# First pass of a gated feed-forward layer made with seven products instead of eight, during attention

## The chip, the cores and the metric

The kernel runs on one core of one Trainium2 chip. The time is device microseconds of one execution, and the figure used is the median of several. A profile of one execution stands beside the times. TensorE multiplies matrices (PE in the profile; PEld is its loading of weights), VectorE (DVE) and ScalarE (ACT) read its results out of PSUM, GpSimd (POOL) works on SBUF alone, and SyncE (SP) issues the transfers.

## The reference

Attention over a window, and its output through a gated layer of two matrix steps. All numbers are fp32.

```python
scores = scale * np.matmul(q, k.transpose(0, 1, 3, 2))     # 8 batches, 8 heads, 576 tokens, 64 per head
mask = (rel >= 0) & (rel < window)                         # window = 128
scores = np.where(mask, scores + bias[None], -1000000000.0)
scores = scores - np.max(scores, axis=-1, keepdims=True)
attn = np.exp(scores)
attn = attn / (np.sum(attn, axis=-1, keepdims=True) + 1e-09)
attn_out = np.matmul(attn, v)

x = attn_out as (4608 tokens, 512)
gate = 1.0 / (1.0 + np.exp(-(x @ w_gate)))                 # w_gate, w_val: 512 x 1536
val = x @ w_val
out = gate * val @ w_out                                   # w_out: 1536 x 512
```

## The kernel before, in words

**How a product is made.** TensorE takes operands in a rounded fp32 form at one column per step. To keep precision each operand is split into a high and a low part (`parts`: a cast, and a subtraction that leaves the rest), and a product of two operands is three matmuls: high by high, high by low, low by high. Weights stand still (128x128), tokens stream past them.

**Three passes over the feed-forward layer.** The 1536 hidden columns are 12 chunks of 128, and each chunk needs a gate half and a value half.

- The *first pass* (`ffn`, matmuls on line 524) makes 4 of the 12 chunks, for all 4608 tokens, in 9 groups of 512. It runs during attention, as soon as a batch's tokens are there, and fills TensorE's gaps. Each group has 4 chunks x 2 halves x 4 input slices x 3 matmuls of 512 columns. It uses two PSUM banks (`mm` 0 and 1) until the last two groups, since the other six hold attention.
- The *second pass* (`ffn2`, line 654) makes the other 8 chunks in groups of 768 tokens. It uses a form with seven products in place of eight: tokens are cut into two halves of 384, the inputs into two, gate and value are the two output halves; sums of the tokens (`low`, `xc`) and sums of the weights (`w2s`, made in `prepare2`) go in, and the results are put together again in PSUM, in SBUF and on the way out.
- The *third pass* (`last`, line 772) is the product with `w_out`, in seven-product form too.

**Attention.** 32 units (a batch and a pair of heads) have 9 blocks of 128 queries each. A block goes through scores on TensorE (line 388), mask and maximum on VectorE (lines 401 and 409), the exponential on ScalarE (line 412), the scaling of the probabilities by the reciprocal sum (lines 432 on ScalarE and 433 on VectorE, in three blocks), a transpose on TensorE (437), a copy to SBUF, a selection on GpSimd (448), and the product with the values (474). Four engines pass each block on.

**What sets the order.** Every instruction is first recorded in a graph (`g.add`) with an engine, a cost, the keys that it reads and writes, and a wish (`want`). `Graph.order` then takes, again and again, the instruction that could start earliest by these costs; ties go to the lower wish. Some instructions have `ways`: other engines that could do them. So the order on each engine is fixed when the program is built, and the engines run it in that order, each waiting where its operands are not there. First-pass TensorE work has the highest wish number, so it goes where nothing else could start; its VectorE and ScalarE work has the lowest, so it goes first where it ties.

**Places of weights.** In `prepare`, the first pass's weights are decoded (they come as 64-bit numbers) and split, 8 pieces. `prepare2` decodes both halves of a chunk, makes the sums and splits seven pieces. Slots 0 to 2 of `w2s` (`KEEP2`) are filled during attention, slots 3 to 7 after it, in memory that attention frees.

Of the kernel before, what the change touches and what calls it, by code (L numbers as in the profile page):

```python
# [8 lines left out]
F32 = mybir.dt.float32  # L9
# [16 lines left out]
NTB = NT // NB  # L26
FC1 = 4
FC2 = NFC - FC1
GRP = 2
N2 = 384  # L30
# [5 lines left out]
KEEP2 = 3  # L36
NPB, NST, NPT, NBOTH = 8, 9, 3, 2
P0, PSTEP = 70.0, 36.0
OUT0, OSTEP = 430.0, 45.0
# [7 lines left out]
W0, WSTEP = 20.0, 2.0  # L47
# [114 lines left out]
def attention_gated_ffn(ctx: ExitStack, tc: tile.TileContext, qd, kd, vd, wg, wv, wo, out):  # L162
# [45 lines left out]
    def keep(tag, *shape):  # L208
        n, (t, a) = 1, spare.get(tag) or (moe.tile([P, (2 if tag[0] == "h" else KC) * 2 * N2], F32, tag=tag, name=f"early_{tag}"), 0)
# [46 lines left out]
    PIECE = 3  # L256

    def piece(z):
        t = T(moe, f"first{z // PIECE}", [P, PIECE * NB], F32R, tag=f"ar{z // PIECE}")
        return t[:, z % PIECE * NB:(z % PIECE + 1) * NB]  # L260

    xpart = lambda part_, c: piece(part_ * KC + c)

    class First:
        name, fcs = "w1", list(range(FC1))

        def at(self, kind, part_, i):
            return 2 * KC + 4 * i + 2 * "gv".index(kind) + part_

        def tile(self, kind, part_, i):  # L270
            return piece(self.at(kind, part_, i))

    class Later:
        name, fcs = "w2", list(range(FC1, NFC))

        def tile2(self, i, part_):
            return T(moe if i < KEEP2 else pools["w2"], f"w2s{i}{part_}", [P, 7, 2 * P], F32R)

    def piece_keys(a):
        keys = [(x, c) for x in ("xhi", "xlo") for c in range(KC)]  # L280
        keys += [("w1", kind, p, i) for i in range(FC1) for kind in "gv" for p in range(2)]
        return keys[a * PIECE:(a + 1) * PIECE]

# [31 lines left out]
    def prepare(w, src, kind, i, want):  # L315
        sb = bitn[0] % 2
        bitn[0] += 1
        bits = lambda: T(moe, f"wbits{sb}", [P, DM], I32)
        kb = ("wbits", sb)
        decode(src, w.fcs[i], bits, kb, want)  # L320
        parts(lambda: w.tile(kind, 0, i), lambda: w.tile(kind, 1, i), lambda: as32(bits()), DM, [kb],
              (w.name, kind, 0, i), (w.name, kind, 1, i), want)


# [16 lines left out]

    slots = {"kr": keep("h2", TOK), "qr": keep("xr", (NBLK + 1) // 2, P)}
    kept = [keep("h2", TRI, P), keep("xr", TRI, P)]

    def slot(x, u, shape):
# [255 lines left out]
    def ffn2(t, w):  # L603
# [89 lines left out]
        for i in range(n):  # L693
            chunk(i)
# [225 lines left out]
```

## Time and profile before

| | us |
|---|---|
| median of 3 runs (lowest, highest) | 1022.73 (1022.44, 1022.83) |
| the profiled execution's own time | 1022.25 |
| its span | 1020.5 |
| TensorE busy | 1002.6 |
| VectorE busy | 752.7 |
| ScalarE busy | 517.7 |
| GpSimd busy | 114.6 |

TensorE's granted clock is 1.00 in every stretch. A busy time is the union of an engine's instructions; the mean of one instruction overlaps the start of the next by some 0.09 us on VectorE and 0.1 us on ScalarE, so how long an instruction keeps its engine is read from the distance between starts. The stretches are: attention with the first pass between its pieces (0 to 308 us), the rest of the first pass (308 to 404), the second pass (404 to 762) and the third (762 to the end).

### The profile page before, as it was taken

What the parts mean: (1) busy time and instruction counts of PE and PEld (TensorE: products, weight loads), DVE (VectorE), ACT (ScalarE), POOL (GpSimd) and SP (SyncE); (2) the same over time, 40 slices, a digit from 0 to 9 for tenths busy, and PEclk for the clock granted to TensorE, in tenths of its full rate; (3) what the DMA queues carried; (4) which work ended last, traced back from release to release, by engine and by line L of the source; (5) the groups of instructions that cost most, each with busy time, mean ns of one, the idle gap of its engine ahead of it and who ended that gap; (6) DMA issues with size and microseconds to landing.
All of it is one profiled execution on the core that took longest, in us unless ns stands there. A gap on an engine that the chain in (4) does not pass through costs nothing.

```text
span 1020.5 us, 17801 instructions
## 1 busy us (share of the span) xinstructions
PE 1002.6 (98%) x6168; PEld 923.2 (90%) x6168; DVE 752.7 (74%) x1969; ACT 517.7 (51%) x1390; POOL 114.6 (11%) x205
## 2 busy tenths in 40 slices
PE   9899899999999999999999999999999999999998
PEld 7677678788787888999999999999999999999998
DVE  8999799877847836568494957747379887879773
ACT  6899888767753322335353534434335434334341
POOL 2343344233330000000000000000000000000000
PEclk9999999999999999999999999999999999999999
DMA  8777677756434324334343443525886354552501
GB/s 289 250 250 266 215 247 238 270 178 202 154 119 148 133 93 145 129 124 160 125 160 137 160 153 119 176 109 200 292 297 209 101 171 133 162 158 91 186 16 63
DMA packets 85865, 174.17 MB, mean 171 GB/s; under 512 B 8208, under 2 KB 52112, under 8 KB 85776
## 3 DMA queue, kind: packets, MB, share of 16 engines
q1 hardware_dynamic: 85776, 173.04, 50.1%
q8 instruction: 48, 0.79, 0.3%
q14 instruction: 41, 0.34, 0.1%
HBM read 114.82 MB, written 58.20 MB: 170 GB/s over the span
## 4 chain that ended last, share of the span: by engine, by line
PE 87%; ACT 5%; DVE 5%; DMA 1%; issue 1%; SPq 0%; ACTq 0%; DVEq 0%
PE mm L654 34%; PE mm L772 25%; PE mm L524 16%; PE mm L474 4%; PE mm L388 4%; PE mm L437 3%; ACT pb L412 2%; DMA qr<-in_q_dram 1%; DVE mm L401 1%; DVE first L192 1%; ACT both L183 1%; DVE pb L409 1%; ACT pb L432 1%; ACT early_xr L412 0%; DMA kr<-in_k_dram 0%
## 5 line engine op out<-in xcount | busy, mean ns | idle before, releaser
L654 PE MATMUL mm<-xc,w2s 128*128 128x384 f32 x2016 | 350.1, 334 | 0.0
L654 PEld LDWEIGHTS mm<-xc,w2s 128*128 128x128 f32 x2016 | 349.4, 188 | 0.5 <-ACT low L183 0.4
L772 PE MATMUL mm<-duo,wo 128*128 128x384 f32 x1512 | 262.7, 334 | 0.5 <-DVE duo L192 0.5
L772 PEld LDWEIGHTS mm<-duo,wo 128*128 128x128 f32 x1512 | 262.1, 188 | 0.8 <-DVE duo L192 0.8
L524 PE MATMUL mm<-first,first 128*128 128x512 f32 x846 | 214.2, 399 | 1.8 <-DVE first L192 1.4
L524 PEld LDWEIGHTS mm<-first,first 128*128 128x128 f32 x846 | 153.2, 188 | 33.6 <-DVE first L192 2.3
L448 POOL TENSOR_SCALAR_AFFINE_SELECT pt<-both 128x384 f32<-128x384 f32 x192 | 106.9, 581 | 191.1 <-ACT both L183 181.3
L665 ACT ACTIVATE sg<-mm 128x384 f32<-128x384 f32 x96 | 47.3, 492 | 122.5 <-PE mm L654 74.5
L661 DVE TENSOR_TENSOR mm<-mm,low 128x384 f32<-128x384 f32 x96 | 54.3, 565 | 74.5 <-PE mm L654 73.6
L412 ACT ACTIVATE pb<-pb,st 128x128 f32<-128x128 f32 x216 | 84.5, 397 | 7.3 <-DVE st L409 7.0
L183 ACT COPY low<-mm 128x384 f32<-128x384 f32 x95 | 45.8, 482 | 65.2 <-PE mm L654 54.6
L474 PEld LDWEIGHTS mm<-pt,vr 128*64 128x64 f32 x832 | 61.2, 137 | 12.8 <-issue 8.3
L192 DVE TENSOR_TENSOR duo<-rows,duo 128x768 fp32r<-128x768 f32 x66 | 62.9, 957 | 9.9 <-ACT duo L183 6.9
L474 PE MATMUL mm<-pt,vr 128*64 128x256 f32 (+2 forms) x832 | 67.4, 306 | 0.6 <-POOL pt L448 0.6
L183 ACT COPY both<-mm 128x384 f32<-128x384 f32 x96 | 45.8, 477 | 37.6 <-PE mm L437 27.6
L401 DVE COPY_PREDICATED mm<-early_h,mm 128x256 f32<-128x256 int32 (+1 forms) x144 | 49.3, 392 | 8.9 <-PE mm L388 8.4
L388 PE MATMUL mm<-kr,qr 64*128 64x256 f32 (+1 forms) x396 | 55.1, 381 | 0.3 <-DMA kr<-in_k_dram 0.3
L183 ACT CAST duo<-rows 128x768 fp32r<-128x768 f32 x45 | 37.0, 834 | 34.1 <-issue 19.3
L543 DVE SCALAR_TENSOR_TENSOR early_hs<-sg,mm 128x512 f32<-128x512 f32 x36 | 24.6, 685 | 38.5 <-PE mm L524 23.9
L409 DVE CUSTOM_DVE_ANT_0 pb<-mm,early_h 128x128 f32<-128x128 f32 x216 | 51.4, 282 | 0.0
L388 PEld LDWEIGHTS mm<-kr,qr 64*128 64x128 f32 x396 | 38.1, 186 | 9.5 <-issue 2.4
L437 PE MATMUL mm<-ident,pb 128*128 128x128 f32 x216 | 38.2, 284 | 7.9 <-ACT both L183 6.1
(116 smaller groups left out, 1073.1 us busy)
## 6 DMA issues: line engine op xcount, KB each, us to landing
hid<-later_hs SPq DMA_DIRECT2D x48, 384.0 KB, 2.4
rows<-hid SPq DMA_DIRECT2D x48, 384.0 KB, 4.1
kr<-in_k_dram SPq DMA_DIRECT2D x21, 576.0 KB, 4.2
wo<-stash_o SPq DMA_DIRECT2D x12, 896.0 KB, 7.1
vr<-in_v_dram SPq DMA_DIRECT2D x32, 288.0 KB, 3.3
xs<-xt SPq DMA_DIRECT2D x32, 288.0 KB, 2.9
stash_o<-wtmp SPq DMA_DIRECT2D x12, 768.0 KB, 3.4
rows_xr<-hid SPq DMA_DIRECT2D x24, 384.0 KB, 3.5
```

Of the source, the lines that this page charges most:

```text
L183: g.add("ACT", act_cost(n, psum), lambda: nc.scalar.copy(out(), src()), reads, writes, want, release=release, ways=[("DVE", dve_cost(n, ps ...
L192: g.add("DVE", dve_cost(n, psum, True), lambda: nc.vector.tensor_tensor(out(), a(), b(), op=ALU.subtract), reads, writes, want, port=not p ...
L388: nc.tensor.matmul(sp[bank_of(r, a)][:, a % 2, lo:], qraw(u)[rows, i // 2], kraw(u)[rows, (i - 1) * P + lo:(i + 1) * P], start=True, stop= ...
L401: g.add("DVE", dve_cost((a1 - a0) * P, psum=True), lambda b=b, a0=a0, a1=a1: nc.vector.copy_predicated(sp[b][:, a0:a1, P:], before[:, a0:a ...
L409: g.add("DVE", 0.21, lambda: nc.vector.tensor_tensor_reduce(pb()[:, e], sp[b][:, a, P:], relm[u.p][:, w], op0=ALU.add, op1=ALU.min, scale= ...
L412: g.add("ACT", 0.39, lambda: nc.scalar.activation(pb()[:, e], pb()[:, e], AF.Exp, bias=st()[:, e:e + 1], scale=-1.0, accum_out=st()[:, 3 + ...
L437: nc.tensor.transpose(tp[:, e], pb()[:, e], ident)
L448: nc.gpsimd.affine_select(pt(u)[:, f0:f0 + 2 * n - 1:2, :], both(), [[0, n], step], cmp, 0.0, base=0, channel_multiplier=mult)
L474: nc.tensor.matmul(to()[e * D:(e + 1) * D, a - e * S - t0:b - e * S - t0], vraw(u)[:, c], seen, start=first, stop=last, skip_group_check=True)
L524: nc.tensor.matmul(mm[s], w.tile(kind, wi, i)[:, c * P:(c + 1) * P], xpart(x, c), start=(k == 0 and c == 0), stop=(k == 2 and c == KC - 1))
L654: nc.tensor.matmul(mm[b][:, 0:N2], w.tile2(i, wp)[:, wk, c * P:(c + 1) * P], combo(k, xp)[:, c], start=(start and c == 0 and j == 0), stop ...
L772: nc.tensor.matmul(mm[b][:, 0:N2], wo2(2 * q + m, wp)[:, k, j * P:(j + 1) * P], duo(xp)[:, m], start=(k in (0, 3, 1) and q == 0 and m == 0 ...
```

## The change

The first pass gets the seven-product form. `ffn` and `prepare` go; `ffn2` serves both passes. For a group of 512 tokens (`N1` = 256 in each half) and a chunk there are now seven products of six matmuls with 256 columns, 42 in place of 24 with 512. Four weight slots hold the sums of chunks 0 to 3: slots 0 to 2 of `w2s`, and a fourth, "e", in the memory (`cells`) that the second pass uses for its token sums. That memory also holds a ring of eight token sums (`ROOM`), of which a group takes seven, so that the next group's first one can be made early. Three results of a chunk share two PSUM banks as halves (`halves`); banks 2 to 7 join for the last two groups. A result is copied or read out between products that go into the same half: products 0, 4, 5 and 6 into one, 1 into the second, 3 and 2 into the third.

Slots 0 to 2 are thus taken until the first pass ends. The second pass starts with slots 3 to 7 (`turn`), and 0 to 2 are filled again meanwhile. No second-pass weights are made during attention any more; the four chunks of the first pass are due at 10, 30, 50 and 70 us. The scaling of probabilities may also go to GpSimd, and its cost on VectorE is put at 0.26 in place of 0.16. Batch 0's output goes straight into the first group's rows.

```diff
-FC1 = 4
-GRP = 2
-P0, PSTEP = 70.0, 36.0
-OUT0, OSTEP = 430.0, 45.0
-W0, WSTEP = 20.0, 2.0
+N1, N2 = 256, 384
+EARLY = 4
+ROOM = 8
+KEPT = 3
+OUT0, OSTEP = 440.0, 45.0
+W0, WSTEP = 10.0, 20.0
...
             g.add("ACT", 0.3, lambda args=args: nc.scalar.mul(*args()), [(kst, 6)], [(kpb, e)], want,
-                  ways=[("DVE", 0.16, True, lambda args=args: nc.vector.tensor_scalar_mul(*args()))])
+                  ways=[("DVE", 0.26, True, lambda args=args: nc.vector.tensor_scalar_mul(*args())),
+                        ("POOL", 0.35, True, lambda args=args: nc.gpsimd.tensor_scalar_mul(*args()))])
...
-        def project(kind, i):
-            s = bank()
-            for c in range(KC):
-                def three(c=c):
-                    for k, (wi, x) in enumerate(((0, 0), (1, 0), (0, 1))):
-                        nc.tensor.matmul(mm[s], w.tile(kind, wi, i)[:, c * P:(c + 1) * P], xpart(x, c),
-                                         start=(k == 0 and c == 0), stop=(k == 2 and c == KC - 1))
...
+    def halves():
+        n = turns[0]
+        turns[0] += 1
+        a, b = pairs[n % len(pairs)]
+        return (a, n % 2), (b, 0), (b, 1)
+
+    def sums_of(fc, want, release):
...
+        decode(wg, fc, gt, kg, want, release)
+        decode(wv, fc, lambda: tt()[:, 0:2].rearrange("p a f -> p (a f)").bitcast(I32), kt, want, release)
...
+        for o, a, b in ((t[0], v0, g0), (t[1], v1, t[0]), (t[2], v1, v0), (t[3], g1, t[1])):
+            minus(o, a, b, 2 * P, [kg], [kt], want)
...
-    def ffn2(t, w):
+    def ffn2(t0, n, w, todo, F):
+        early = n == N1
+        spots = halves if early else (lambda: [(bank(), 0) for _ in range(3)])
...
+            for k in MADE:
+                at[k] = ringed[0] % ROOM
+                ringed[0] += 1
...
             def product(k, b, start):
                 def six():
                     for c in range(2):
                         for j, (xp, wp) in enumerate(((0, 0), (0, 1), (1, 0))):
-                            nc.tensor.matmul(mm[b][:, 0:N2], w.tile2(i, wp)[:, wk, c * P:(c + 1) * P], combo(k, xp)[:, c],
+                            nc.tensor.matmul(bk(b)(), w.part(i, wp, k, k + 1)[:, 0, c * P:(c + 1) * P], combo(k, xp)[:, c],
...
+            for step in (first, second, fourth, third) if early else (first, third, fourth, second):
+                step()
...
+    slot1 = [*range(KEPT), "e"]
+    turn = [*range(KEPT, NRES), *range(KEPT)]
...
-            for k, (src, kind, i) in enumerate(todo):
-                prepare(w1, src, kind, i, W0 + WSTEP * k)
+            for fc, i in enumerate(slot1):
+                prepare2(sums, i, fc, W0 + WSTEP * fc)
...
-                ffn(todo1.pop(0), w1)
+                if early[0] == LATE:
+                    pairs.extend((b, b + 1) for b in (2, 4, 6))
...
+                ffn2(early.pop(0) * 2 * N1, N1, sums, [(i, fc) for fc, i in enumerate(slot1)], FIRST)
...
-    for i in range(KEEP2):
-        prepare2(w2, i, 2.0e6 + i, P0 + PSTEP * i)
...
+    for i in turn:
+        prepare2(sums, i, held[i], FIRST + 0.5)
```

The order that comes out of it, at three places. First TensorE in a late unit of attention, where first-pass matmuls lead up to the product with the values (`mm` 6 and 7 are the names that end in 152 and 153); before:

```order
L437 MATMUL mm_152<-ident,pb_224 128x128 x3
L524 MATMUL mm_147<-first_412,first_597 128x512 x2
L524 MATMUL mm_147<-first_583,first_597 128x512
L474 MATMUL mm_153<-pt_469,vr_184 64x256
L474 MATMUL mm_153<-pt_469,vr_184 64x192
L474 MATMUL mm_153<-pt_469,vr_184 64x256 x4
```

and with the change (`cells` are the token sums, `w2s` the weight sums):

```order
L603 MATMUL mm_147<-cells_530,w2s_423 128x256
L603 MATMUL mm_147<-cells_530,w2s_441 128x256
L603 MATMUL mm_147<-cells_983,w2s_423 128x256
L603 MATMUL mm_147<-cells_530,w2s_423 128x256
L603 MATMUL mm_147<-cells_530,w2s_441 128x256
L603 MATMUL mm_147<-cells_983,w2s_423 128x256
L449 MATMUL mm_153<-pt_477,vr_184 64x256
L449 MATMUL mm_153<-pt_477,vr_184 64x192
```

Pieces of three matmuls with 512 columns have become pieces of six with 256. Over the whole order, 450 of 864 first-pass matmuls stood ahead of the end of attention (the last product with the values), and now 804 of 1512 do.

Second, VectorE behind the last scores of attention, where the rest of the first pass and the preparation of slots 3 to 7 meet; one chunk's piece of it, in the new order (`L610` and `L618` read out a chunk's results, `L289`, `tt` and `w2s` prepare weights, `cells` and `low` are token sums):

```order
L183 CAST w2s_4216<-tt 128x1280
L286 TENSOR_SCALAR wbits_523<-wbits_523 128x512
L610 TENSOR_TENSOR mm_147<-mm_147,low 128x256
L191 TENSOR_TENSOR w2s_4247<-tt,w2s_4216 128x1280
L610 TENSOR_TENSOR mm_147<-mm_147,low 128x256
L289 SCALAR_TENSOR_TENSOR wbits_523<-wraw_191,wbits_523 128x512
L610 TENSOR_TENSOR later_hs_1144<-mm_146,later_hs_1144 128x256
L618 SCALAR_TENSOR_TENSOR later_hs_1144<-sg_1014,mm_147 128x256
L191 TENSOR_TENSOR cells_1039<-low,cells_991 128x512
L286 TENSOR_SCALAR tt<-tt 128x512
L570 TENSOR_TENSOR low<-low,rows 128x512
L618 SCALAR_TENSOR_TENSOR later_hs_1144<-sg_1242,later_hs_1144 128x256
```

Before, a chunk had one such read (`L543`) there; now it has five, with the next group's token sums and the weights of two slots between them. From the last scores to the first token sum of the second pass VectorE had 105 instructions and has 197.

Third, GpSimd in the middle of attention; before:

```order
L448 AFFINE_SELECT pt_346<-both_245 128x3x128 x2
L448 AFFINE_SELECT pt_469<-both_266 128x3x128 x2
L448 AFFINE_SELECT pt_469<-both_245 128x3x128 x2
L448 AFFINE_SELECT pt_469<-both_266 128x3x128 x2
L191 TENSOR_TENSOR w2s_2026<-tt,w2s_2011 128x1280
```

and with the change:

```order
L423 AFFINE_SELECT pt_477<-both_247 128x3x128 x2
L408 TENSOR_SCALAR pb_228<-pb_228,st_456 128x128 x2
L423 AFFINE_SELECT pt_477<-both_268 128x3x128 x2
L408 TENSOR_SCALAR pb_292<-pb_292,st_219 128x128 x2
L423 AFFINE_SELECT pt_477<-both_247 128x3x128 x2
```

The scalings stand between the selections. Of the 288 scalings, VectorE had 145 and ScalarE 143; now GpSimd has 172, ScalarE 116 and VectorE none.

More of the change, by code (lines that the diff above doesn't have):

```diff
@@ L252, in attention_gated_ffn, with cells, part @@
     g.warm = warm
[L256 to L282, printed above, removed]
+    def cells(z, p=0, n=2):
+        t = T(moe, f"cells{z // 3}", [P, 3 * NB], F32R, tag=f"ar{z // 3}")
+        return t[:, z % 3 * NB + p * 2 * P:z % 3 * NB + (p + n) * 2 * P]
+    class Sums:
+        def part(self, s, p, a, b):
+            if s == "e":
+                z = 2 * ROOM + a // 2 + 3 * p if a < 6 else 2 * ROOM + 6
+                return cells(z, p if a == 6 else a % 2, b - a).rearrange("p (a f) -> p a f", f=2 * P)
+            return T(moe if s < KEPT else pools["w2"], f"w2s{s}{p}", [P, 7, 2 * P], F32R)[:, a:b]
     raws, mms, banks = [0], [0], [2]
@@ L486, in values @@
-        move(lambda: xs[u.b][u.p], xt, [("xt", u.s, t0) for t0, _, _ in spots], [("xs", u.b, u.p)], want, S / 2)
+            at0 = u.b == 0 and t0 == 0
+            dst = first if at0 else lambda t0=t0, t1=t1: xt()[:, t0:t1]
+            kx = [("xr", u.p // 2, (h, e)) for h in range(2) for e in range(2)] if at0 else [("xt", u.s, t0)]
+            copy(dst, lambda t0=t0, t1=t1, to=to: to()[:, 0:t1 - t0], t1 - t0, [key], kx, want, psum=True)
+            if u.b == 0:
+                move(lambda t0=t0, t1=t1: xs[0][u.p][:, t0:t1], dst, kx, [("xs", 0, u.p), ("xs", 0, u.p, t0)], want, (t1 - t0) / 2)
@@ L574, in prepare2 @@
+    def prepare2(w, i, fc, want, release=0.0):
+        pool = ["w2pool"] if i in range(KEPT, NRES) else []
+        two, five, kg, kt = sums_of(fc, want, release)
+        cuts = [(2, 7)] if i != "e" else [(2, 4), (4, 6), (6, 7)]
+        todo = [(0, 2, two, kg)] + [(a, b, lambda a=a, b=b: five()[:, a - 2:b - 2], kt) for a, b in cuts]
+        for a, b, src, k in todo:
+            parts(lambda a=a, b=b: w.part(i, 0, a, b), lambda a=a, b=b: w.part(i, 1, a, b), src, (b - a) * 2 * P,
                   [k, *pool], ("w2", i, 0, a), ("w2", i, 1, a), want)
@@ L804, in attention_gated_ffn @@
         load(units[n])
+    sums = Sums()
+    slot1 = [*range(KEPT), "e"]
+    turn = [*range(KEPT, NRES), *range(KEPT)]
+    held = {i: EARLY + n for n, i in enumerate(turn)}
+    early = list(range(NT1))
+    LATE = (B - 1) * S // (2 * N1)
     at = 0
```

263 lines of the change are left out of this document (109 added, 154 removed).

## The prediction

> **What bounds the kernel now.** I read the busy time of each engine in stretches first, then the chain of work that ended last, then the groups of instructions. The stretches (columns: TensorE, its weight loads, VectorE, ScalarE, GpSimd, granted clock, DMA share, GB/s):
>
> ```profile
> 0.00:70.00 70.00, 63.99 (x498) 49.58 (x500) 63.08 (x329) 57.91 (x230) 22.78 (x46) 1.00 0.79 265
> 70.00:175.00 105.00, 99.86 (x769) 78.51 (x767) 92.48 (x417) 89.86 (x337) 46.51 (x75) 1.00 0.71 241
> 175.00:308.00 133.00, 131.96 (x967) 106.38 (x964) 95.07 (x481) 93.84 (x349) 43.03 (x82) 1.00 0.55 185
> 308.00:404.00 96.00, 94.75 (x416) 77.77 (x417) 60.11 (x97) 30.64 (x49) 0.00 (x0) 1.00 0.38 127
> 404.00:762.00 358.00, 358.00 (x2065) 357.54 (x2064) 239.06 (x398) 147.60 (x291) 2.32 (x3) 1.00 0.47 168
> ```
>
> TensorE is the bound from about 175 us to the end. Up to there all three engines are near 90%, and the chain of waits runs through ScalarE, VectorE and two loads. From 308 us the rest of the first pass runs alone, with VectorE at 63%. The chain (start, length, what):
>
> ```profile
> 7.70 2.87 PE mm L250 x24
> 79.55 5.37 DMA qr<-in_q_dram
> 114.08 0.55 PE mm L437 x3
> 167.44 5.02 DMA qr<-in_q_dram
> 305.91 2.01 PE mm L474 x24
> 316.82 87.01 PE mm L524 x382
> 403.82 347.74 PE mm L654 x2004
> ```
>
> From 316.82 us on it is matmuls without a break. A 512-column matmul takes 87.01/382 = 0.2278 us, a 384-column one 347.74/2004 = 0.1735 us. Line 524's matmuls alone, by stretch:
>
> ```profile
> 0.00:308.00 308.00, 121.73 (x451) 79.28 (x452) 1.00 0.66 222
> 308.00:404.00 96.00, 94.58 (x414) 77.25 (x414) 1.00 0.38 127
> ```
>
> So just over half of the first pass is done during attention, and 414 matmuls come after it.
>
> **The change: TensorE.** The two distances give 0.424 ns a column and 10.7 ns fixed, so 256 columns take 0.1192 us. Bounds: half of a 512-column matmul, 0.1139, and no less than a 384-column one, 0.1735, if loading weights were to set the pace. I take 0.1192: the warm-up matmuls on line 250 follow each other at 2.87/24 = 0.1196 us with a weight load each, so a load of 128 columns fits into that. The first pass goes from 864 x 0.2278 = 196.8 us to 1512 x 0.1192 = 180.2: 16.6 us less (24.6 less, or 65.5 more, at the bounds). By the order this falls into two parts. Ahead of the end of attention there were 450 matmuls (102.5 us) and are now 804 (95.8): 6.7 less. Behind it there were 414 (94.3) and are 708 (84.4): 9.9 less.
>
> **What it adds elsewhere.** Reads, sums and splits become more and shorter. The groups:
>
> ```profile
> L543 DVE SCALAR_TENSOR_TENSOR early_hs<-sg,mm 128x512 f32<-128x512 f32 x36 | 24.6, 685 | 38.5 <-PE mm L524 23.9 <-issue 14.6
> L535 ACT ACTIVATE sg<-mm 128x512 f32<-128x512 f32 x36 | 21.4, 596 | 41.7 <-PE mm L524 41.2
> L183 ACT CAST first<-early_xr 128x512 fp32r<-128x512 f32 x20 | 12.2, 619 | 6.9 <-PE mm L524 6.5
> L665 ACT ACTIVATE sg<-mm 128x384 f32<-128x384 f32 x96 | 47.3, 492 | 122.5 <-PE mm L654 74.5 <-DVE mm L661 47.9
> L183 ACT COPY low<-mm 128x384 f32<-128x384 f32 x95 | 45.8, 482 | 65.2 <-PE mm L654 54.6 <-DVE mm L661 8.4 <-ACT later_hs L183 2.1
> L432 ACT ACTIVATE pb<-pb,st 128x128 f32<-128x128 f32 x103 | 34.1, 401 | 1.3 <-DVE st L429 0.6 <-DVE st L427 0.4
> L302 ACT ACTIVATE wbits<-wraw 128x512 f32<-128x512 f32 x22 | 14.9, 676 | 2.8 <-DVE w2s L192 1.3 <-DMA wraw<-in_moe_w_gate_dram 1.2 <-DMA wraw<-in_moe_w_out_dram 0.2
> L433 DVE TENSOR_SCALAR pb<-pb,st 128x128 f32<-128x128 f32 x113 | 28.5, 301 | 0.5
> masks.py:199 POOL TENSOR_SCALAR_AFFINE_SELECT ident<-ident 128x128 f32<-128x128 f32 x1 | 0.3, 292 | 0.1
> L191 POOL TENSOR_TENSOR tt<-tt,wbits 128x256 f32<-128x256 f32 x1 | 0.7, 734 | 51.0 <-DVE tt L306 51.0
> L183 ACT CAST xc<-later_xr 128x768 fp32r<-128x768 f32 x23 | 19.2, 835 | 5.8 <-PE mm L524 3.7 <-PE mm L654 1.7
> L192 DVE TENSOR_TENSOR xc<-later_xr,xc 128x768 fp32r<-128x768 f32 x30 | 28.7, 956 | 0.7 <-ACT xc L183 0.2
> ```
>
> and VectorE back to back, where the distance of starts is what an instruction costs its engine (start, length):
>
> ```profile
> 318.48 0.43 DVE L303 TENSOR_SCALAR tt<-tt 128x512 int32<-128x512 int32 x1
> 318.82 0.43 DVE L303 TENSOR_SCALAR wbits<-wbits 128x512 int32<-128x512 int32 x1
> 319.15 0.69 DVE L306 SCALAR_TENSOR_TENSOR tt<-wraw,tt 128x512 int32<-128x512 int32 x1
> 319.75 0.69 DVE L306 SCALAR_TENSOR_TENSOR wbits<-wraw,wbits 128x512 int32<-128x512 int32 x1
> ...
> 322.96 0.42 DVE L192 TENSOR_TENSOR tt<-tt 128x256 f32<-128x256 f32 x1
> 323.30 0.42 DVE L192 TENSOR_TENSOR tt<-wbits,tt 128x256 f32<-128x256 f32 x1
> 323.75 0.83 DVE L184 CAST w2s<-tt 128x1280 fp32r<-128x1280 f32 x1
> 324.62 1.49 DVE L192 TENSOR_TENSOR w2s<-tt,w2s 128x1280 fp32r<-128x1280 f32 x1
> 326.02 0.68 DVE L543 SCALAR_TENSOR_TENSOR early_hs<-sg,mm 128x512 f32<-128x512 f32 x1
> ```
>
> That is 0.34 us for 512 columns with one input, 0.60 with two, 0.34 for 256 with two, 0.87 for the wide cast, 1.40 for the wide subtraction. On ScalarE I take 0.1 us off the means: 0.50 for a tanh of 512, and by the slope between 512 and 384 0.29 for one of 256 and 0.28 for a copy; 0.52 for a cast, 0.30 for a scaling, 0.58 for a decode.
>
> *Up to 175 us* (the first 18 units). By the order ScalarE gets 18 more casts (+9.4), 18 copies (+5.0), 12 short tanhs for 7 long ones (0), 19 fewer scalings (-5.7), 5 fewer copies for the transposes (-1.9), 3 fewer decodes and one wide cast less (about -2.9): 3.9 us more. VectorE comes out level, since all its scalings go (145, 44 us by the mean of line 433). GpSimd takes 172 of them. No row shows that operation there; the nearest is its 128x128 selection, 0.29 us, so 50 us; above lies a two-input operation on 256 columns, 0.73 us, 126 us in all. GpSimd's queue holds the selections that the products with the values wait for; busy 112 of 308 us, it has room for either, and a selection comes at most one piece of scaling later. Six of the 14 loads of first weights (512 KB each) leave attention: 3.1 MB, 13 us of transfer at 241 GB/s, in a stretch whose chain holds two query loads of 5 us each. SP gets a dozen more transfers in all, and idles mostly. So the attention stretch may end up to 6.7 us sooner (if TensorE's saving counts in full) or 3.9/0.9 = 4.3 us later (if ScalarE, at 85 to 90%, sets the pace). I take 0.
>
> *From the last scores to the second pass.* VectorE has 197 instructions there: 64 of 512 with two inputs (38.4), 102 of 256 (34.7), 6 wide subtractions (8.4), 3 wide casts (2.6), 14 of 512 with one input (4.8), and a few small: 89 us, where TensorE has 810 x 0.1192 = 96.6 plus two products with the values (2.0 each) and five groups of transposes (0.5 each), 103 in all. It fits, but it is not spread evenly: by the same prices ten successive chunks behind attention hold 56.8 us of VectorE's work, and 10 x 42 x 0.1192 = 50.1 of TensorE's. VectorE runs in order, so these chunks go at its pace: 6.7 us lost, and not won back where it has less to do. The work is that of slots 3 to 7, which was there before too, under 0.60 us of reads a chunk instead of 1.7 and fewer sums. Before, this stretch lost 1.25 us (96.0 less 94.75): credit 1.2.
>
> *Into the second pass.* Its token sums lie where the ring is, so each waits for a product of the last chunk, a cast and a subtraction (0.84 and 0.96 us in the second pass's own groups). The order puts other chunks' products between; I take 1 us, between 0 and 3. Slots 0 to 2 are filled under the second pass's first group: 47 us on VectorE in its 58 us of matmuls, hidden. If that cover went it would be one chunk late, 7 us. The second and third passes have the same instructions: 0.
>
> Sum: 0 - 9.9 - 1.2 + 6.7 + 1.0 = -3.4 us. Made against the profiled execution, 1022.25 us (span 1020.5, 1.75 around it), that is 1018.9; the median of the runs is 0.5 above it, so **1019 us**. Own range 1014 to 1023.
>
> **The rivals.**
>
> *Everything lands* (TensorE sets the pace throughout, VectorE's preparations fit between): -6.7 - 9.9 - 1.2, so 1005, range 1003 to 1012. For it: the stretch 175 to 308 is at 99% on TensorE and 71% on the others. Against: the ten chunks above.
>
> *Late reads: slower.* Four times a chunk TensorE writes again to a half that was read just before: behind products 0, 4, 3 and 5, with one product between. That product lasts 6 x 0.1192 = 0.715 us; before, the second pass had 6 x 0.1735 = 1.04 us for the same, and its matmuls had 0.0 us idle. That only says that hand-over plus a 0.482-us copy fit into 1.04, so the hand-over is under 0.56; now 0.715 less a copy of 0.378 leaves 0.34. Each read may thus be late by 0 to 0.22 us, and more where it stands behind a preparation. Among attention's matmuls this is covered; behind attention, in 17 chunks, 68 reads are not. At 0.15 us each it costs 10 us more: 1029, range 1025 to 1036. It turns the change into a loss from 0.05 us each (3.4/68). My sum has it at nothing, because the rows do not show the hand-over.
>
> *The gain goes in attention*: ScalarE's 4.3 us come in full, the tail wins 3.4: 1023 to 1024, no change.
>
> *Weight loads show* (0.188 us between 256-column matmuls, the mean of a load in its row below): 1512 x 0.188 = 284, +87, 1110.
>
> ```profile
> L654 PEld LDWEIGHTS mm<-xc,w2s 128*128 128x128 f32 x2016 | 349.4, 188 | 0.5 <-ACT low L183 0.4
> L250 PEld LDWEIGHTS mm<-ident 128*128 128x128 f32 x80 | 10.7, 216 | 2.1 <-POOL ident masks.py:199 1.4 <-issue 0.7
> ```
>
> Against it: matmuls already follow at 0.1735 and 0.1196 with loads as long as that. The Trainium skill, TensorE: Matmul & The Clock Gate, states in "Measured speedup vs the span model" that a weight load overlaps a running matmul only where the row groups differ, and in "LDWEIGHTS (loading the stationary operand)" that it takes the columns over 1.2 GHz, 107 ns here. By that a 256-column matmul would come every 214 ns (an estimate), and the time would be about 1149. By that rule 384 columns would need 267 ns; the trace shows 173.5 and disagrees.
>
> **How the numbers follow.** Chances: the forecast 0.41, late reads 0.32, gain gone in attention 0.14, everything lands 0.11, weight loads 0.02. The range for 8 in 10 leaves out the weight loads and most of the far ends of the two outer cases: 1007 to 1030. What a measurement of this kernel tells from no change is about 0.2%, 2 us. Faster by more: all of "lands" and 0.36 of the forecast, 0.47. Within: the rest of the forecast, 0.05, and the gain gone in attention, 0.14: 0.19. Slower: 0.34.
>
> **What would show it.** Right: line 603's 256-column matmuls 0.119 us apart; the last product with the values near 306 us; VectorE above 90% in the 50 us behind it and TensorE idle 6 to 9 us there, released by VectorE; the second pass starting near 400 us. Late reads: TensorE idle behind attention over 15 us in many small waits on copies and totals. Gain gone in attention: the last product with the values after 310 us. Lands: no idle time behind attention. The forecast is wrong if the second pass starts before 394 or after 406 us, or if its own 358 us change.

## The result and the profile after

The changed kernel takes **1057.6 us** (median; 1056.1 to 1060.5) against 1022.8 for the kernel before: a ratio of **1.034**, with a 95% interval of 1.033 to 1.036. It is slower by 3.4%; the prediction was 1019 us, its range 1007 to 1030. The profiled execution has a span of 1058.7 us, 38.2 more than before.

Where the 38.2 us came in is read from the timeline view, which gives the first and the last start of a group of matmuls (last two numbers of the time columns). Before, line 474 is the product with the values and line 654 the second pass:

```profile
L474 PE MATMUL mm<-pt,vr x832: 219/326/430, 19.1 to 307.7; 128*64 128x256 f32 x65, 128*64 128x64 f32 x64, 128*64 128x192 f32 x26, 128*64 128x128 f32 x12
L654 PE MATMUL mm<-xc,w2s x2016: 333/334/444, 403.7 to 754.4; 128*128 128x384 f32 x184
```

After, lines 449 and 603, and the last row holds short matmuls of the first pass:

```profile
L449 PE MATMUL mm<-pt,vr x832: 219/326/431, 19.9 to 329.3; 128*64 128x256 f32 x66, 128*64 128x64 f32 x63, 128*64 128x192 f32 x24, 128*64 128x128 f32 x14
L603 PE MATMUL mm<-xc,w2s x2016: 333/334/443, 437.4 to 792.6; 128*128 128x384 f32 x184
L603 PE MATMUL mm<-cells,cells x370: 274/283/389, 114.4 to 441.5; 128*128 128x256 f32 x185
```

- **Attention** (to the last matmul with the values): 307.7 to 329.3, **21.6 us** more.
- **The tail** (from there to the first matmul of the second pass): 96.0 to 108.1, **12.1 us** more.
- **The second pass**: 350.7 to 355.2, **4.5 us** more, of which about 2 are the 18 short matmuls that stand behind its first one (18 x 0.12).

The third pass is as before. The stretches of the changed kernel (columns as in the prediction: TensorE, its weight loads, VectorE, ScalarE, GpSimd, granted clock, DMA share, GB/s):

```profile
0.00:70.00 70.00, 59.02 (x475) 46.76 (x477) 60.49 (x296) 58.50 (x232) 52.22 (x90) 0.99 0.74 250
70.00:175.00 105.00, 92.48 (x781) 78.44 (x778) 87.85 (x361) 84.59 (x305) 69.03 (x108) 0.97 0.64 210
175.00:308.00 133.00, 128.74 (x1154) 114.41 (x1155) 104.15 (x481) 103.93 (x397) 91.57 (x156) 1.00 0.57 185
329.00:392.00 63.00, 50.40 (x361) 45.07 (x357) 48.04 (x95) 27.40 (x64) 6.96 (x7) 0.97 0.36 114
392.00:437.00 45.00, 43.45 (x342) 41.39 (x341) 42.01 (x84) 27.74 (x66) 6.85 (x6) 1.00 0.53 164
```

In 70 to 175 us the three engines that were near 90% are all less full than before: VectorE went from 92.48 to 87.85, ScalarE from 89.86 to 84.59, TensorE from 99.86 to 92.48. They wait more. Only GpSimd, with the scalings, went up, from 46.51 to 69.03. The tail has two halves that look nothing alike: in 329 to 392 us TensorE idles 12.6 of 63 us, in 392 to 437 us 1.6 of 45. What it waits for in the whole tail (us in total, times, longest):

```profile
PE mm L603 <- ACT sg L614: 4.1, 7, 1.6
PE mm L603 <- ACT low L182: 3.9, 7, 0.8
PE mm L603 <- DVE later_hs L618: 3.5, 5, 0.8
```

and how that looks in the chain of waits (start, length):

```profile
361.55 0.99 PE mm L603 x6
362.57 0.39 ACT sg L614
362.96 0.04 issue
363.00 0.99 PE mm L603 x6
364.09 0.10 DVE mm L610
364.19 0.24 issue
364.43 0.68 DVE cells L191
365.11 0.34 DVE later_hs L618
365.45 0.04 issue
365.50 2.43 PE mm L603 x18
```

A product (six matmuls), then a read of PSUM, then the next product: TensorE stands still while ScalarE or VectorE empties PSUM. The last read here (`later_hs`, line 618) also stands behind the making of a token sum (`cells`, 0.68 us) in VectorE's queue. Before, the same stretch held one unbroken piece of 87 us.

### The profile page after: what moved, and what is told of

Read it like the earlier page. It is cut to its first block, busy times and chain, and to the rows that moved or that the text cites. A ratio compares the mean times of both kernels' runs of the same rounds, so it can differ in the third digit from the quotient of the medians.

```text
span 1058.7 us, 19708 instructions
## 1 busy us (share of the span) xinstructions
PE 1009.5 (95%) x6820; PEld 958.2 (91%) x6820; DVE 812.3 (77%) x2022; ACT 565.2 (53%) x1535; POOL 259.0 (24%) x405
## 4 chain that ended last, share of the span: by engine, by line
PE 78%; DVE 12%; ACT 6%; issue 2%; POOL 1%; DMA 1%; ACTq 0%; DVEq 0%; POOLq 0%; SPq 0%
PE mm L603 44%; PE mm L738 24%; PE mm L362 4%; PE mm L449 4%; PE mm L412 2%; ACT pb L386 2%; DVE mm L375 2%; DVE pb L383 1%; DVE cells L191 1%; ACT sg L614 1%; DVE mm L610 1%; DVE later_hs L618 1%; DVE w2s L191 1%; DVE st L401 1%; DVE low L570 1%
## 5 line engine op out<-in xcount | busy, mean ns | idle before, releaser
L603 PE MATMUL mm<-cells,w2s 128*128 128x256 f32 x1134 | 162.9, 292 | 22.2 <-ACT low L182 7.2
L603 PEld LDWEIGHTS mm<-cells,w2s 128*128 128x128 f32 x1134 | 143.8, 192 | 34.2 <-ACT low L182 10.7
L614 ACT ACTIVATE sg<-mm 128x384 f32<-128x384 f32 (+1 forms) x168 | 74.4, 445 | 147.6 <-PE mm L603 95.9
L610 DVE TENSOR_TENSOR mm<-mm,low 128x384 f32<-128x384 f32 (+1 forms) x168 | 84.8, 505 | 86.1 <-PE mm L603 78.9
L408 POOL TENSOR_SCALAR pb<-pb,st 128x128 f32<-128x128 f32 x172 | 116.1, 689 | 39.1 <-DVE st L403 22.1
L386 ACT ACTIVATE pb<-pb,st 128x128 f32<-128x128 f32 x288 | 113.2, 398 | 13.3 <-DVE st L383 12.7
L182 ACT COPY low<-mm 128x384 f32<-128x384 f32 (+1 forms) x163 | 70.3, 433 | 88.1 <-PE mm L603 70.1
L618 DVE SCALAR_TENSOR_TENSOR later_hs<-sg,later_hs 128x384 f32<-128x384 f32 (+1 forms) x84 | 44.5, 530 | 27.8 <-ACT sg L614 27.5
L610 DVE TENSOR_TENSOR later_hs<-mm,later_hs 128x384 f32<-128x384 f32 (+1 forms) x84 | 41.7, 496 | 22.7 <-ACT later_hs L182 12.1
L603 PE MATMUL mm<-cells,cells 128*128 128x256 f32 x370 | 55.1, 289 | 3.9 <-ACT later_hs L182 1.0
```

Source lines behind the costliest of these rows:

```text
L182: g.add("ACT", act_cost(n, psum), lambda: nc.scalar.copy(out(), src()), reads, writes, want, release=release, ways=[("DVE", dve_cost(n, ps ...
L386: g.add("ACT", 0.39, lambda: nc.scalar.activation(pb()[:, e], pb()[:, e], AF.Exp, bias=st()[:, e:e + 1], scale=-1.0, accum_out=st()[:, 3 + ...
L408: ("POOL", 0.35, True, lambda args=args: nc.gpsimd.tensor_scalar_mul(*args()))])
L603: nc.tensor.matmul(bk(b)(), w.part(i, wp, k, k + 1)[:, 0, c * P:(c + 1) * P], combo(k, xp)[:, c], start=(start and c == 0 and j == 0), sto ...
L610: g.add("DVE", dve_cost(n, psum=True), lambda: nc.vector.tensor_tensor(o(), bk(b)(), a(), op=ALU.add), [ka(b), *reads] if okeys else reads ...
L614: g.add("ACT", act_cost(n, psum=True), lambda: nc.scalar.activation(sg[h](), bk(b)(), AF.Tanh, scale=0.5), [ka(b)], [("sg", h)], F)
```

## The experiments

All take the changed kernel, or one of the others here, as their start. "Attention" below is the time from the first to the last matmul with the values, from the timeline rows: 288.6 us before, 309.4 after. (Where the expectations count from the first to the last product with the values, that is 1.9 us less.) The runs that leave numbers out, and e8, were executed once each. How far one execution can be trusted: the change and e4 below have the same order on TensorE up to the end of attention, and differ there by 0.8 us.

### Is it the scaling on GpSimd?

The group row after the change shows 172 scalings of 0.69 us in the mean, where the prediction had 0.29 and the planner's price is 0.35; the timeline's median is 0.603.

```profile
L408 POOL TENSOR_SCALAR pb<-pb,st 128x128 f32<-128x128 f32 x172 | 116.1, 689 | 39.1 <-DVE st L403 22.1 <-DVE st L383 8.6 <-ACT xt L182 3.6
L408 POOL TENSOR_SCALAR pb<-pb,st x172: 594/603/1595, 10.2 to 319.2; 128x128 f32<-128x128 f32 x172
```

So the first suspect was this part of the change. It was taken away (e1), priced as measured (e2), and put alone into the kernel before (e3).

```diff
 # e1_nopool: no GpSimd way
-  ways=[("DVE", 0.26, ...), ("POOL", 0.35, ...)]
+  ways=[("DVE", 0.26, ...)]
 # e2_truecost
-  ("POOL", 0.35, ...)
+  ("POOL", 0.58, ...)
 # e3_before_pool: the kernel before
-  ways=[("DVE", 0.16, ...)]
+  ways=[("DVE", 0.26, ...), ("POOL", 0.35, ...)]
```

> The change without its GpSimd way for the scalings: ScalarE 198, VectorE 90, GpSimd 0 (the planner's prices for the other two as in the change). Theory G (the scalings on GpSimd cost attention its 21 us): the last product with the values comes near 306 us instead of 327; by the order 750 short matmuls instead of 708 stand behind it, 42 x 0.12 = 5 us more, so about 1042 us. Rival S (the seven-product form's own reads, sums and splits on ScalarE and VectorE cost the 21 us): attention ends at 325 us or later, about 1057 us or more.

> The change with one number altered: the planner's price of a scaling on GpSimd 0.58 us (as measured) instead of 0.35; it then gives GpSimd 38 scalings, VectorE 83, ScalarE 167, and 102 more short matmuls stand behind the last scores (12 us). Theory G, if each scaling on GpSimd costs alike: 38/172 of the 21 us stay, the last product with the values near 310 us, the end near 1057.6 - 16 + 12 = 1053 us. If the wrong price itself (a plan that runs away from the chip) is the cost and not the number of scalings: near 1042 to 1049 us. Rival S: 1057 us or more, with attention ending no sooner.

> The kernel before, with only the change's prices and the GpSimd way for the scalings: none is left on VectorE. Theory G: attention ends 15 to 21 us later than before, with the same first pass behind it, so 1038 to 1044 us. Rival S: 1021 to 1025 us.

| | time, us | ratio to before (95%) | attention | last matmul with the values |
|---|---|---|---|---|
| e1_nopool | 1053.5 | 1.031 (1.029 to 1.032) | 306.8 | 326.6 |
| e2_truecost | 1051.6 | 1.028 (1.027 to 1.030) | 291.9 | 311.2 |
| e3_before_pool | 1020.3 | 0.998 (0.997 to 0.999) | 286.5 | 306.3 |

Theory G fell by e1 and e3. Without any scaling on GpSimd attention is nearly as long as with 172 (with 762 instead of 804 short matmuls in it), and in the kernel before the same move makes it a little faster. Taken alone, e2 came out as theory G had it (last product near 310 us, the end near 1053) and not as rival S did. But it has 702 instead of 804 short matmuls ahead of the end of attention: 12 of the 18 us are work that comes later, with waits, and the whole gains 6 us. What is left is the seven-product form itself (rival S, though e1 is 4 us faster than S had it).

### The tail: how many banks

In the change, groups 7 and 8 of the first pass use four pairs of PSUM banks, all others one pair. e4 records groups 5 to 8 behind all of attention, so that all that is left then has four pairs.

```diff
-    LATE = (B - 1) * S // (2 * N1)      # 7
+    LATE = 5
-            while early and (early[0] + 1) * 2 * N1 <= (u.b + 1) * S:
+            while early and (early[0] + 1) * 2 * N1 <= (u.b + 1) * S and (early[0] < LATE or u is units[-1]):
```

> The change with groups 5 to 8 of the first pass (instead of 7 and 8) recorded behind all of attention, on four pairs of PSUM banks, so that behind attention a half is written again only many products after it was read; the number of matmuls on each side of attention's end is unchanged (804 and 708), and so are the scalings. Theory L (late reads cost the tail about 11 us: its idle waits on copies, tanhs and totals): the stretch from the last values to the second pass goes from 105 to about 95 us, the whole to 1046 to 1050 us. Rival V (VectorE's amount of work sets the tail's pace, whatever the banks): 104 to 106 us, the whole 1055 to 1060 us.

It took **1040.2 us**, 1.017 of before (1.015 to 1.019): 17 us less than the change. Its stretch of the same length and place:

```profile
328.00:391.00 63.00, 61.88 (x504) 59.92 (x500) 58.03 (x122) 39.02 (x91) 8.22 (x7) 1.00 0.48 148
```

504 matmuls in 63 us where the change has 361, with TensorE idle for 1.1 us instead of 12.6. VectorE is at 92% here, so its amount of work is not what set the pace in the change (rival V falls; theory L had 95 us for the tail and 1046 to 1050 in all, so more banks were worth more than it had). The second pass now starts at 417.9 us:

```profile
L603 PE MATMUL mm<-xc,w2s x2016: 331/334/446, 417.9 to 772.7; 128*128 128x384 f32 x184
L449 PE MATMUL mm<-pt,vr x832: 219/326/431, 19.8 to 328.4; 128*64 128x256 f32 x66, 128*64 128x64 f32 x63, 128*64 128x192 f32 x24, 128*64 128x128 f32 x14
```

The tail is 417.9 - 328.4 = 89.5 us, 6.5 less than in the kernel before. The second pass, where 18 short matmuls now stand, takes 4.1 of that back (354.8 us against 350.7): behind attention, with banks enough, the form wins 2.4 us. Attention is untouched, 308.6 us, and now explains all of what is left.

### Why two banks cost so much: whole banks, or the order

A chunk has three regions in its two banks: one half of the first, both halves of the second. Laying the starts and lengths of line 603's matmuls beside the reads on lines 182, 610 and 614, 0 of the 64 reads in 329 to 392 us overlap a matmul on the same bank, and 48 overlap one on the other. Reads and matmuls thus keep apart by whole banks, where the planner's keys go by halves, so its order may count on overlaps that never come. The Trainium skill, PSUM — Partial Sum Buffer, states in "PSUM bank collisions raise a hardware error" that PSUM is to be guarded by bank (and quadrant of partitions), not by address. The trace agrees in that no such overlap is there; what an overlap would do no run here shows. e16 and e17 give the planner the same view.

```diff
-        ka = lambda r: ("ph", *r) if early else ("mm", r[0])
+        ka = lambda r: ("ph", r[0], 0) if early else ("mm", r[0])
```

> The change with one key altered: for the early chunks the planner's accounts go by the whole PSUM bank instead of by its halves, as the waits on the chip do; the matmuls, reads and banks are the same, only the order is made anew (726 short matmuls ahead of the last scores, 786 behind). If the order made without these waits is what loses the time: 1045 us or less. If the waits themselves lose it (two banks for three regions), whatever the order: 1052 to 1060 us, and the first 372 products' matmuls behind attention still take 7 us or more for each 42.

> The same key in the kernel of e4_banks (groups 5 to 8 behind attention on four pairs of banks). If the order is what loses time in attention: below 1035 us. If the waits themselves: 1036 to 1043 us, as e4_banks (1040.2).

1056.6 us (1.033, 1.031 to 1.035) and 1041.1 (1.018, 1.016 to 1.019): no better than without the key. Attention is 14 us shorter in both (295.3 and 294.7 us), but with 726 instead of 804 short matmuls in it, and the tail and the second pass are longer. In e16 the first 372 short matmuls behind attention take 7.2 us for each 42 (7.4 in the change, 5.4 in e4): the waits stay in this other order.

Nor is the sharing of a bank by two halves most of them. With the program's order laid beside the trace of the change, these first 62 products (372 matmuls) start 17.0 us late in sum, counted over the spacing of 0.12. For 15.2 us of it the read that ended last before was one of the very half to be written; for 1.6 us it was one of the other half of that bank. (2.7 of the 15.2 us stand behind reads that began as a product into the other half ended, so the bank may have a share in these.) What is too small is the room as a whole, one pair of banks, which e4 shows; what waits by halves would give in the same room was not run.

e9 joined e2's price to e4's banks, as the two gains looked separate.

> e4_banks and e2_truecost together: groups 5 to 8 behind attention on four pairs of banks, and the planner's price of a scaling on GpSimd 0.58 us. If the two effects are separate, the last product with the values comes near 309 us as in e2_truecost, and the tail runs without late reads: 810 x 0.12 = 97 us and some 7 us more, so the second pass starts near 412 us and the end is 1033 to 1036 us. If the waits only move elsewhere: 1039 us or more.

It took 1040.3 us, as e4 alone. Attention ends 17 us sooner (311.2), but 102 more short matmuls then stand behind it (12 us), and the second pass begins only 3.7 us sooner (414.2) with 30 of them still to come. It lasts 358.7 us, 3.9 more than in e4. The waits moved elsewhere.

### Attention: taking single kinds of work away

The next six leave e4's order as it is. Five shorten or leave out one kind of instruction (in e5, e6 and e11 for groups 0 to 4 of the first pass, shown in short below), and e8 puts 18 more warm-up matmuls into TensorE's gaps.

```diff
 # e5_short_reads: copies, tanhs, totals and products with the gate, each
-  ... bk(b)() ...
+  ... bk(b)()[:, 0:32] ...
 # e6_short_products: of each six matmuls one is left
+  if early and t0 < LATE * 2 * N1 and not (c == 0 and j == 2): continue
 # e7_no_scaling_act
-  lambda args=args: nc.scalar.mul(*args())
+  lambda args=args: None
 # e8_warm
-  WARM = 30.0
+  WARM = 70.0
 # e10_short_pool
-  nc.gpsimd.tensor_scalar_mul(pb()[:, e], ...)
+  nc.gpsimd.tensor_scalar_mul(pb()[:, e, 0:32], ...)
 # e11_short_sums: casts, subtractions and sums of groups 1 to 4, each
-  val()
+  val()[:, :, 0:32]
```

> The kernel of e4_banks, its order unchanged, with the PSUM reads of the seven-product chunks of groups 0 to 4 (three copies and two tanhs on ScalarE, three totals and two products with the gate on VectorE for each chunk) made on 32 columns instead of 256: the numbers of these tokens are left out. About 19 such chunks lie in attention, so this takes off about 19 x 5 x 0.19 = 18 us on ScalarE and 19 x 5 x 0.23 = 22 us on VectorE. Theory R (the added reads on these two engines are what attention waits for): the last product with the values comes at 306 to 316 us instead of 326. Rival T (TensorE's own matmuls and their spacing): 322 us or later.

> The kernel of e4_banks, its order unchanged, with one of the six matmuls of each product of groups 0 to 4 (the rest of these products is left out): some 134 products lie in attention, so TensorE has 134 x 5 x 0.12 = 80 us less to do there. Theory R: attention still ends after 312 us. Rival T: it ends before 300 us.

> The kernel of e4_banks, its order unchanged, without the 116 scalings of probabilities that ScalarE has (these probabilities are left unscaled): 116 x 0.30 = 35 us less on ScalarE in attention, and nothing less in the reads of the products. Theory A (ScalarE's load as a whole is what attention waits for): the last product with the values comes 12 us or more sooner, before 314 us. Rival Q (the products wait for their own reads, which stand in the queues of both engines behind other work, so that load elsewhere matters little): less than 5 us sooner.

> The kernel of e4_banks with TensorE's idle gaps filled by warm-up matmuls up to 70 us instead of 30. Granted clock in 60 to 80 us was 0.93 and 0.90 there. Theory C (the gaps let the clock fall, and that costs attention time): clock 1.00 up to 80 us and the last product with the values 2 to 3 us sooner. Rival: the same clock, or the same end.

> The kernel of e4_banks, its order unchanged, with GpSimd's 172 scalings made on 32 columns instead of 128 (the other probabilities are left unscaled). Theory G (that one of these takes 0.58 us where the order was written for 0.35 delays attention): the last product with the values comes 6 us or more sooner, at 320 us or before, and GpSimd's busy time falls by 40 us or more. Rival: GpSimd has room, as the prediction said, and the end moves by less than 2 us.

> The kernel of e4_banks, its order unchanged, with the token sums and splits of groups 1 to 4 made on 32 of 256 columns in each half (seven casts, seven subtractions and four sums for each group; the rest of these operands is left as it was): about 8 us less for each group over ScalarE, VectorE and GpSimd, 30 us in all. If the added sums count as the added reads do: the last product with the values 6 to 10 us sooner (316 to 320 us). If they hide: less than 3 us.

| against e4_banks (308.6 us, to 328.4) | attention | difference | its end |
|---|---|---|---|
| e5, reads on 32 columns | 297.9 | -10.7 | 321.2 |
| e11, sums and splits on 32 columns | 304.4 | -4.2 | 325.0 |
| e7, no scalings on ScalarE | 303.4 | -5.2 | 323.4 |
| e10, GpSimd's scalings on 32 columns | 306.8 | -1.8 | 325.5 |
| e6, one matmul of six | 306.8 | -1.8 | 326.6 |
| e8, warm-up matmuls to 70 us | 307.4 | -1.2 | 327.2 |

```profile
L453 PE MATMUL mm<-pt,vr x832: 219/326/431, 23.3 to 321.2; 128*64 128x256 f32 x66, 128*64 128x64 f32 x63, 128*64 128x192 f32 x24, 128*64 128x128 f32 x14
L449 PE MATMUL mm<-pt,vr x832: 219/326/689, 19.8 to 326.6; 128*64 128x256 f32 x67, 128*64 128x64 f32 x62, 128*64 128x192 f32 x25, 128*64 128x128 f32 x13
```

The first row is e5's, the second e6's. e5, e13, e14 and e15 fill some buffers at the start. In e5 and e15 that puts the first six products with the values 3.5 us later than in e4, all alike, and the time from first to last leaves that out. By their ends alone the effects are smaller: 7.2 us for e5. Three of the six fell between their two expectations: e5 ended attention later than theory R had it (306 to 316 us) and sooner than rival T did (322), e10 moved the end by 2.9 us (6 or more against under 2), and e11 by 3.4 (6 to 10 against under 3).

The plainest row is e6. Its stretches show TensorE with a fifth of its time free, and attention ends 1.8 us sooner for it:

```profile
70.00:175.00 105.00, 80.14 (x549) 61.67 (x548) 85.06 (x350) 81.99 (x296) 66.03 (x105) 0.81 0.62 202
175.00:308.00 133.00, 108.22 (x805) 84.91 (x803) 106.04 (x490) 105.64 (x402) 94.85 (x161) 0.87 0.59 191
```

TensorE's work does not set the pace there (rival T falls; part of what it saves goes into a lower clock: its busy time in 0 to 330 us fell from 302.0 to 264.8 us, 37 and not the 80 of the count). Nor does ScalarE's load as such: some 35 us less on it (e7) gave 5.2, against 12 or more by theory A and under 5 by rival Q, while 17 us less on ScalarE and 21 on VectorE in the reads gave 10.7. e7 won its 5 us before the 17th product with the values and nothing behind it; e5 wins all along. GpSimd, for all that its scalings cost twice the price, has nearly the room that the prediction gave it (e10). The warm-up matmuls did keep the granted clock at 1.00 (40 to 100 us; 0.97 in e4), but that is worth 1.2 us and not 2 to 3. Two engines or one? e14 and e15 shorten the reads of one engine each, e13 joins e5, e10 and e11.

> The kernel of e4_banks, its order unchanged, with the shortenings of e5_short_reads, e10_short_pool and e11_short_sums together (the same numbers are left out). Counted from the first product with the values, which a fill of five buffers at the start moves by some 3 us: if the named causes are separate and account for the delay, the last product with the values is 16 to 20 us nearer to the first than in e4_banks (306.7 us there), 287 to 291 us, close to the 286.7 us of the kernel before. If they overlap and something else is the wait: 293 us or more.

> The kernel of e4_banks, its order unchanged, with only ScalarE's five reads of each chunk of groups 0 to 4 on 32 columns (its copies and tanhs; these numbers are left out). From the first to the last product with the values 306.7 us in e4_banks, 296.0 in e5_short_reads. If ScalarE's reads carry the delay: 299 us or less. If VectorE's do: 304 us or more. If both engines take turns in one chain: between, about 301.

> The kernel of e4_banks, its order unchanged, with only VectorE's five reads and products with the gate of each chunk of groups 0 to 4 on 32 columns (these numbers are left out). If VectorE's reads carry the delay: 299 us or less from the first to the last product with the values. If ScalarE's do: 304 us or more. If both engines take turns: about 301.

Attention took 304.9 us with ScalarE's reads short (-3.7), 303.7 with VectorE's (-4.9): both count, and together more (-10.7) than the sum. (By the ends: -1.7, -1.4 and -7.2.) Jointly (e13) it took 293.0 us, 15.6 less, near the sum of the three parts (16.7); by the expectation's count that is 291.1, at the edge of its 287 to 291. The stretch looks like the kernel before again, with TensorE at 99%:

```profile
L453 PE MATMUL mm<-pt,vr x832: 219/326/690, 20.7 to 313.7; 128*64 128x256 f32 x65, 128*64 128x64 f32 x64, 128*64 128x192 f32 x25, 128*64 128x128 f32 x13
175.00:308.00 133.00, 132.17 (x1200) 119.61 (x1199) 80.18 (x487) 93.23 (x402) 70.71 (x165) 1.00 0.56 181
```

Of the 20.0 us by which e4's attention is longer than that of the kernel before, about 15.6 are thus named; 4.4 are not. (By the ends, 14.7 of 20.7.) The reads and sums are made short here, not taken away: what is left of them may hold some of the rest, which no run shows.

### Both forms in one kernel

If reads and sums are what attention cannot carry, the eight-product form belongs in it and the seven-product form behind it. e12 does that.

```diff
+        eight = early and t0 < LATE * 2 * N1
+        if eight:      # four splits of 512 tokens; per chunk 24 matmuls of 512 columns,
+            ...        # one tanh and one product with the gate, in banks 0 and 1
```

> Both forms in one kernel: groups 0 to 4 of the first pass with the eight products of the kernel before (two PSUM reads a chunk, four casts and four subtractions a group; the halves of v that the seven-product sums lack are kept in cells of the ring that this form leaves free), groups 5 to 8 with seven products on four pairs of banks behind attention; scalings on GpSimd as in the change. If the reads and sums of the seven-product form are what attention waits for, attention ends where it did in e3_before_pool or sooner (300 to 306 us), and the rest of the first pass is shorter than there by an eighth of the work of groups 5 to 8: 16 chunks x (24 x 0.2278 - 42 x 0.12) = 7 us, less 2 to 5 us into the second pass: 1014 to 1020 us. If attention does not win: 1025 us or more.

It took 1022.7 us (0.9996 of before, 0.999 to 1.001): between the two forecasts, and no gain. Attention is 275.5 us long, 33.1 less than in e4, though the first-pass matmuls in it are nearly as much work (405 x 0.2278 = 92.3 us against 804 x 0.12 = 96.5). So it is the form that attention could not carry. TensorE is never idle from 175 us on:

```profile
L449 PE MATMUL mm<-pt,vr x832: 219/326/430, 20.1 to 295.6; 128*64 128x256 f32 x65, 128*64 128x64 f32 x63, 128*64 128x192 f32 x25, 128*64 128x128 f32 x14
175.00:295.00 120.00, 120.00 (x908) 96.91 (x906) 75.42 (x393) 85.31 (x325) 90.08 (x163) 1.00 0.57 186
295.00:399.00 104.00, 99.34 (x734) 93.03 (x731) 94.23 (x184) 57.21 (x129) 11.74 (x11) 1.00 0.45 150
```

Against the kernel before, attention is 13.1 us shorter, but 10.3 of these are work put off: 405 long matmuls instead of 450 stand ahead of its end. Behind it 75 of them are still to come (17 us), TensorE idles 4.7 us with VectorE at 91%, and 30 short matmuls run inside the second pass, which lasts 356.5 us instead of 350.7. Of the kernels here that leave nothing out, only e3_before_pool is faster than the kernel before, by 0.2%.

## Why the prediction was wrong

**TensorE's price: right.** The short matmuls follow each other at a median of 0.120 us (from the starts of line 603's), predicted 0.1192; the weight loads, 0.188 to 0.192 us each, do not show (rival at 1110). The rule by which the prediction had 1149, that a load overlaps a running matmul only where the row groups differ, stands in the Trainium skill, TensorE: Matmul & The Clock Gate, in the section "The mechanism"; this spacing disagrees with it. Line 603 up to 329 us, in the stretches of that line alone, is busy for 5.7 us less than the 121.73 us of line 524, near the 6.7 computed:

```profile
sum 329.00, PE 116.05 PEld 100.97; mean PE 38.68 PEld 33.66
```

**"Up to 175 us ... I take 0", with bounds of -6.7 and +4.3: wrong, +21.6.** This is the step that failed most. Its counts were fair: up to the start of the 19th product with the values (171.4 us before, 186.2 after; the second row stops at 186.0) the busy time is

```profile
0.00:171.40 171.40, 160.25 (x1226) 124.85 (x1226) 152.21 (x729) 144.18 (x552) 66.30 (x118) 1.00 0.74 250
```

```profile
0.00:186.00 186.00, 162.28 (x1348) 134.93 (x1349) 156.16 (x701) 151.84 (x570) 127.86 (x209) 0.98 0.68 224
```

so 4 us more on VectorE, where level was forecast, and 8 on ScalarE, where 3.9 was. But 14.8 us more went by. A chunk has nine reads of PSUM now and a product with the gate in SBUF, and had two reads. Each takes some 0.4 us and stands in an in-order queue among attention's own work. The prediction turned busy time into delay by dividing by the share of one engine. It also summed only up to 175 us, and took the rest of attention as covered by the 71% of the other engines; the other 6.8 us came in there. The joint experiment gives reads, sums and GpSimd's scalings 15.6 us. Our reading is that no single engine is the bound in that stretch, and that each read is one more stop in a chain that passes through all of them, which busy time does not price; that neither TensorE's work (e6) nor ScalarE's load (e7) alone moves much fits this, but no run shows the chain by itself.

**GpSimd's scaling at 0.29 us: twice as dear (0.60), and yet "GpSimd has room" held**: 1.8 us (e10). A wrong price in the right step.

**"These chunks go at its pace: 6.7 us lost": not seen in the change, near in e4.** In the change the late reads cover it. In e4 VectorE is at 92% over 63 us, as forecast, and the matmuls behind attention start 6.6 us later in sum than at 0.12 each (before: 1.4 later than at 0.228). The windows count only 2.5 us of that as idle, since the first matmul after a wait reads longer (0.38 us in place of 0.28, and the next one starts 0.22 us after it). That VectorE's amount of work makes these 6.6 us is not shown. From the end of attention to the end of the second pass e4 wins 2.4 us where the sum had 3.4: that part was near, once the late reads are gone.

**Late reads at nothing in the sum: wrong, and the rival had the mechanism in part.** It was priced as 68 reads of 0 to 0.22 us, more behind a preparation, 1029 us in all at 0.15. Two sizes were off. Only the part of the tail in the one pair of banks is hit: the first 336 short matmuls behind attention took 7.65 us for each 42, the later ones 5.5 (from their starts), so some 36 reads and not 68. And each is late by (7.65 - 5.5)/4 = 0.54 us. It is also not the four products that the rival named (4, 5, 2 and 6): of the 17.0 us above, products 4, 1 and 3 have 5.0, 4.6 and 4.3, and the other four 3.1 together. Product 4 waits for the copy of product 0, as the rival had it; product 1 mostly for the tanh, and product 3 for the product with the gate, of the chunk before in the same half. With four pairs e4 has a tail 18.6 us shorter (17 us in all). This turned the forecast gain in the tail of some 4 us into a loss of 12.1.

**"I take 1 us, between 0 and 3" into the second pass: 2.3 us** besides the 18 matmuls that moved into it (2.2 us). VectorE is busy for 40.9 of the 42.6 us from 437.4 on, where the prediction called 47 of 58 us hidden; TensorE loses 1.1 us there. Mis-sized, but small.

Of the marks that the prediction set, "the last product with the values near 306" and "the second pass starting near 400" were both missed (327 and 437), and VectorE above 90% in the 50 us behind it too (48.0 of 63 us). The last product after 310 us was the mark of the gain gone in attention, which was priced at 4.3 us. TensorE idle over 15 us behind attention in small waits was the mark of late reads, and it reads 14.2 us by the two rows above.

## What to carry to other kernels

A form with fewer multiplications paid here only where TensorE is the bound: count the PSUM reads, sums and splits that it adds, and ask stage by stage who carries them; in an attention that passes through four engines in turn, shares of 80 to 90% left no room for nine reads in place of two. Count how soon each piece of PSUM is written again, and what else stands ahead of its read in the reading engine's queue: with one pair of banks 42 matmuls took 7.4 us here, with four pairs 5.4. When the order changes, compare how much work stands on each side of a mark before calling a stretch shorter. To see whether an engine sets the pace of a stretch, shorten its work in an unchanged order and look at the end of the stretch (a fifth of TensorE's time set free moved it by 1.8 us here), rather than at its busy share.

## What had not been expected of the hardware

- A scaling of 128x128 on GpSimd takes 0.603 us in the median, as long as its selection of three such blocks:

```profile
L423 POOL TENSOR_SCALAR_AFFINE_SELECT pt<-both 128x384 f32<-128x384 f32 x192 | 107.6, 585 | 60.6 <-ACT both L182 55.3 <-PE mm L603 2.1 <-DVE both L183 1.8
```

  The Trainium skill, GPSIMD Engine Reference, section "Engine selection", puts one-input work on GpSimd at roughly line rate; here the same operation on VectorE was 0.301 in the mean before, so the trace disagrees by a factor of two.
- The granted clock reads lower in 70 to 175 us where TensorE idles in many short waits: 0.97 with 92.5 of 105 us busy, 0.81 with 80.1 (e6), 1.00 with 99.9 (before). The busy share alone does not set it: 0.97 stands also beside 50.4 of 63 us (329 to 392, the change).
- Taking five sixths of the matmuls out of the products, some 80 us of TensorE's work by the count (134 x 5 x 0.12) and 37 us of its busy time, moved the end of attention by less than 2 us.
